# A third tile put ahead of the second halves of the first two, its predecessor's x parked in DRAM, and a new order for the opening

## The chip, the cores and the metric

The kernel runs on one core of a Trainium2 chip. The metric is the device time of one execution in microseconds. TensorE (PE in the rows) multiplies matrices, ScalarE (ACT), VectorE (DVE) and GpSimd (POOL) work on elements, and SyncE (SP) does nothing but issue transfers, in the order of its queue.

## The reference

Three layers follow each other: attention inside chunks of 64 tokens, a layer h·cos(h) of width 2048, and a layer with a softmax gate and a norm of width 1024.

```python
# attention: 8 batches, 8 heads, 576 tokens, head size 64, chunks of 64 tokens
scores = scale * np.matmul(q_c, k_c.transpose(0, 1, 2, 4, 3))
attn = exp(scores - max); attn = attn / (sum(attn) + 1e-09)
x = (attn @ v_c)  ->  4608 tokens x 512
# first layer
h = x @ w_in                     # 512 -> 2048
y = (h * np.cos(h)) @ w_out      # 2048 -> 512
# second layer
h = y @ w_in                     # 512 -> 1024
solu = h * softmax(h)
out = ((solu - mean) / sqrt(var + 1e-06) * g_ln) @ w_out
```

The weights come as 64-bit floats, so that the kernel has to make 32-bit values of them first.

## The kernel before

**Tiles and steps.** The 4608 tokens are 9 tiles j of 512. The first layer is 16 slices f of 128 columns a tile, and a step is one (tile, slice): 144 steps in all. The list `blocks` sets their order: slices 0 to 7 of tile 0, the same of tile 1, then slices 8 to 15 of tile 0, of tile 1, and from step 32 on tile after tile. The sum of a half tile goes to DRAM (`y_part`) and is fetched again (`load_part`) when the second half is done. Halving the first two tiles lets work begin while only half of the weights have been turned into 32-bit values.

**A step.** Every product is made of three passes over a high and a low half of each operand. In a step, PE does 12 products `h` (from `xh`, `xl` and `whi`, `wlo`), ACT rounds h to whole turns (`kt`), DVE takes the rest (`r`), ACT does sine and square (`r<-r`), DVE makes `g`, ACT its high half `gh` and DVE its low half `gl`, and two steps later PE does 12 products `y` out of gh and gl. The first 8 steps use full 32-bit products in place of gh and gl (`gf`).

**Attention.** The tokens are cut into units: 0 to 3 are 128 tokens each (tile 0), all later ones 256, two a tile. Units 0 to 3 are the opening: for each unit q and k are loaded (word `lt`), transposed on PE (`Tq`, `Tk`, tile `qkt`) and copied by ACT (`Cq`, `Ck`), then scores on PE (`S`, tile `sc`), maximum and difference on DVE (`M`, `U`), exponential on ACT (`E`), sums and scaling (`R`, `L` on DVE or `Lp` on POOL), transposes on PE (`P`, tile `pt`) with a copy on ACT (`D`), and the product with v (`V`, tile `x`), which ACT and DVE split into xh and xl (`XH`, `XL`). The word `n` followed by a number is that many products of the identity with itself (tile `none`); nothing reads them.

**The order.** Up to step 33 the whole program is one list of words, written out by hand; each engine does its share of the words in the list's order and never passes one by. From step 34 on a function `step(n)` gives the order, with slots `e`, `p1`, `y`, `a1`, `d1`, `p2`, `a2`, `d2` in which other work is hung by `plan(n, slot, what)`: step n does `mm_in(n)`, slot e, `kt` and `r` of n, `gh` and `gl` of n-1, p1, `mm_out(n-2)`, y, a1, d1, sine and `g` of n, p2, a2, d2. The units of a later tile are hung at step j·16-18 and j·16-10; the scores of a unit and the loads of the next one (`load_next`: 16 transfers for q, 16 for k) are two steps later in slot p2, and its product with v and four loads of the next v nine steps later in p1 (or eight later in p2).

**The blocks of the second layer's weights.** Two halves kk of the second layer's first weights are loaded (`load_blk`) and made into seven blocks. `keep` writes a block's high half (ACT, `wk<-wf` or `wk<-z`) and low half (DVE) into one of the two halves e of the tile `wk`, and stores them to DRAM from SP's queue (`w_w<-wk`, `w_s<-wk`). The next block with the same e can be written only when that store is through. The order is w12 (e=0), w11 (1), w22 (0), s1 (1), s2 (0), s3 (1), s4 (0).

Of the kernel before, what the change touches and what calls it, by code (L numbers as in the profile page):

```python
# [11 lines left out]
F32 = mybir.dt.float32  # L12
F32R = mybir.dt.float32r
# [15 lines left out]
def kernel(  # L29
# [13 lines left out]
    B, H, S, D = q.shape  # L43
# [3 lines left out]
    P = 128  # L47
    CH = 64
    T = 512
    NJ = NT // T  # L50
    SUB = T // P
    NI = NT // P
    KD = DM // P
    NF = F1 // P
# [8 lines left out]
    dr = ctx.enter_context(tc.tile_pool(name="dr", bufs=1, space=DRAM))  # L63
# [10 lines left out]
    NB = 8  # L74

    N32 = NB
    blocks = [(0, 0, NB), (1, 0, NB), (0, NB, NF), (1, NB, NF)]
    blocks += [(j, 0, NF) for j in range(2, NJ)]
    steps = [(j, f) for j, f0, f1 in blocks for f in range(f0, f1)]
    heads = {(j, f0) for j, f0, f1 in blocks}  # L80
    tails = {(j, f1 - 1) for j, f0, f1 in blocks}
    y_part = [dr.tile([P, KD * T], F32, name=f"yp{j}") for j in range(2)]
    y_dram = [dr.tile([2, P, 7 * 256], F32, name=f"yd{j}") for j in range(NJ)]

    xp = ctx.enter_context(tc.tile_pool(name="xp", bufs=2))
# [27 lines left out]
    sync = InOrder(nc.sync, in_order_loads)  # L113
# [110 lines left out]
    def load_w2in(g):  # L224
        t = sp_.tile([P, 1024], U64, tag="st", name="st")
        sync.dma_start(out=t, in_=w_in2[g * P:(g + 1) * P, :])
        raw["in2", g] = t
# [29 lines left out]
    def load_blk(kk):  # L257
        t = sp_.tile([P, 2048], F32, tag="st", name="wf")
        sync.dma_start(out=t, in_=w2f[kk])
        blk[kk] = t, zp.tile([P, 1024], F32, tag="z", name="z"), sp_.tile([P, 2048], F32R, tag="st", name="wk")  # L260
# [144 lines left out]
    def warm(n):  # L405

        t = ps_h.tile([P, P], F32, tag="h", name="none")
        for _ in range(n):
            pe.matmul(out=t, lhsT=ident, rhs=ident, start=True, stop=True)

    def att_tok(i, w):

# [170 lines left out]
    xh, xl = {}, {}  # L583
# [102 lines left out]
    def load_part(j):  # L686
        t = sp_.tile([P, KD, T], F32, tag="st", name="yp")
        sync.dma_start(out=t.rearrange("p m t -> p (m t)"), in_=y_part[j])
        parts[j] = t
# [75 lines left out]
    if True:  # L765
# [48 lines left out]
        for i in range(SUB, NU):  # L814
            j, o = divmod(UNITS[i][0] * CH, T)
# [3 lines left out]
        def plan(n, when, what):  # L819
            att.setdefault((n, when), []).append((lambda i: what(), NU))  # L820

        def conv_at(key, places):
            for (e, k), (n, when) in zip(((0, 0), (0, 1), (0, 2), (1, 0), (1, 1), (1, 2)), places):
                plan(n, when, lambda e=e, k=k: conv(key, e, k))

        for t in (2, 3):
            o = NF * t
            for x in range(2):
                plan(o + 5, "p2", lambda g=2 * x + t - 2: load_w2in(g))
            conv_at(("in2", t - 2), ((o + 7, "a2"), (o + 8, "d2"), (o + 9, "d2"), (o + 8, "a2"), (o + 10, "d1"), (o + 12, "d1")))  # L830
            conv_at(("in2", t), ((o + 13, "a1"), (o + 13, "d1"), (o + 13, "d2"), (o + 13, "a2"), (o + 14, "d2"), (o + 16, "d1")))
        for t in (4, 5):
            o, kk = NF * t, t - 4
            plan(o + 5, "p2", lambda kk=kk: load_blk(kk))
            for what, key, e, n, x in (
# [3 lines left out]
            ):  # L839
                if what == "s":  # L840
                    plan(o + n, f"d{x}", lambda kk=kk, key=key: blk_sum(kk, key))
                else:
                    plan(o + n, f"a{x}", lambda kk=kk, key=key, e=e: keep(kk, e, key, 0))
                    plan(o + n, f"d{x}", lambda kk=kk, key=key, e=e: keep(kk, e, key, 1))
        for t in (6, 7):
            o = NF * t
            for x in range(2):
                g = 2 * (t - 6) + x
                plan(o + 5, "p2", lambda g=g: load_w2out(g))
            g = 2 * (t - 6)  # L850
# [11 lines left out]
        def half_out(n, m):  # L862
# [20 lines left out]
            "Ck": lambda i: att_tokc(i, 1), "S": att_qk, "M": att_max, "U": att_sub, "E": att_exp,  # L883
            "R": att_sum, "L": att_mul, "P": att_pt, "D": att_ptc, "V": att_pv,
            "XH": lambda i: att_x(i, 0), "XL": lambda i: att_x(i, 1),
            "n": warm,
            "nq": lambda i: att_nat(i, "q"), "nk": lambda i: att_nat(i, "k"),
            "cq": lambda i: att_natc(i, "q"), "ck": lambda i: att_natc(i, "k"),
            "tq": lambda i: att_tr(i, "q"), "tk": lambda i: att_tr(i, "k"),
# [223 lines left out]
        BEFORE = 34  # L1113
        ordered[0] = True
        for word in (
# [26 lines left out]
        ).split():  # L1142
            if word == "|":
                first.close()
                cp = act_a.enter_context(tc.tile_pool(name="cp", bufs=2, reuse_waits="tile"))
            else:
                say(word)
# [20 lines left out]
        for n in range(BEFORE - 1, END):  # L1168
            j, f = steps[n - LAG]
# [46 lines left out]
        for i in range(EARLY, NI // 2 + (LAG2 + 1) // 2 + 1):  # L1216
            p, t = i - 1, 2 * i - LAG2
# [98 lines left out]
```

## Time and profile before

| what | value |
|---|---|
| median of 3 runs | 1256.03 us (1254.58 to 1257.68) |
| the profiled execution | 1254.68 us, of which its span is 1252.9 us |
| TensorE busy in the span | 1241.4 us (99%) |
| mean granted TensorE clock | 0.998 |
| VectorE, ScalarE busy | 862.4 us (69%), 751.7 us (60%) |

The span goes from the first to the last instruction; the rest of the profiled execution's time lies around it. A busy engine is not one at its peak, and the ends of TensorE's instructions are modelled, so that starts are compared with starts below.

### The profile page before, as it was taken

What the parts mean: (1) busy time and instruction counts of PE and PEld (TensorE: products, weight loads), DVE (VectorE), ACT (ScalarE), POOL (GpSimd) and SP (SyncE); (2) the same over time, 40 slices, a digit from 0 to 9 for tenths busy, and PEclk for the clock granted to TensorE, in tenths of its full rate; (3) what the DMA queues carried; (4) which work ended last, traced back from release to release, by engine and by line L of the source; (5) the groups of instructions that cost most, each with busy time, mean ns of one, the idle gap of its engine ahead of it and who ended that gap; (6) DMA issues with size and microseconds to landing.
All of it is one profiled execution on the core that took longest, in us unless ns stands there. A gap on an engine that the chain in (4) does not pass through costs nothing.

```text
span 1252.9 us, 20476 instructions
## 1 busy us (share of the span) xinstructions
PE 1241.4 (99%) x7636; PEld 1012.5 (81%) x7636; DVE 862.4 (69%) x1390; ACT 751.7 (60%) x1108; POOL 130.0 (10%) x216
## 2 busy tenths in 40 slices
PE   8999999999999999999999999999999999999998
PEld 7767888888888888888888888888888888888887
DVE  5968875666766766667667757647689777777761
ACT  5968865555645645646646547537666655656552
POOL 1213322011011011011011011000000000000010
PEclk9999999999999999999999999999999999999999
DMA  9952152463263254354373371561556543454325
GB/s 226 276 138 101 58 135 57 114 171 74 54 176 66 58 144 128 85 136 130 80 169 76 85 160 51 194 221 60 164 142 180 129 125 108 121 152 122 75 50 120
DMA packets 249476, 153.95 MB, mean 123 GB/s; under 512 B 180001, under 2 KB 223521, under 8 KB 247585
## 3 DMA queue, kind: packets, MB, share of 16 engines
q1 hardware_dynamic: 245824, 148.32, 45.8%
q0 software_dynamic: 3456, 4.20, 1.5%
q8 instruction: 60, 0.98, 0.4%
q14 instruction: 40, 0.32, 0.1%
q10 hardware_dynamic: 96, 0.13, 0.0%
HBM read 85.73 MB, written 41.68 MB: 102 GB/s over the span
## 4 chain that ended last, share of the span: by engine, by line
PE 96%; ACT 1%; SPq 1%; DMA 1%; DVE 0%; issue 0%; ACTq 0%; DVEq 0%
PE h L104 44%; PE y L104 32%; PE o L104 15%; PE sc L104 2%; PE x L104 2%; SPq L104 1%; DMA qki<-in_k 0%; PE none L104 0%; PE kt L431 0%; PE qt L431 0%; PE pt L104 0%; DMA yd<-ye 0%; PE qkt L104 0%; SPq L1063 0%; ACT lh L104 0%
## 5 line engine op out<-in xcount | busy, mean ns | idle before, releaser
L104 PE MATMUL h<-xh,whi 128*128 128x512 f32 x576 | 229.4, 399 | 0.1
L104 PE MATMUL h<-xl,whi 128*128 128x512 f32 x576 | 224.0, 390 | 0.0
L104 PE MATMUL h<-xh,wlo 128*128 128x512 f32 x576 | 223.9, 390 | 0.0
L104 ACT ACTIVATE kt<-h 128x512 int32<-128x512 f32 x144 | 85.7, 595 | 225.6 <-PE h L104 224.6
L104 PE MATMUL y<-gh,whi 128*128 128x512 f32 x544 | 212.6, 391 | 0.0
L104 PE MATMUL y<-gl,whi 128*128 128x512 f32 x544 | 211.7, 389 | 0.0
L104 PE MATMUL y<-gh,wlo 128*128 128x512 f32 x544 | 211.7, 389 | 0.0
L104 ACT ACTIVATE r<-r 128x512 f32<-128x512 f32 x288 | 181.7, 631 | 47.5 <-DVE r L104 42.9
L104 DVE SCALAR_TENSOR_TENSOR r<-kt,h 128x512 f32<-128x512 int32 x144 | 98.6, 685 | 151.1 <-ACT kt L104 150.9
L104 DVE SCALAR_TENSOR_TENSOR g<-r,h 128x512 f32<-128x512 f32 x136 | 92.7, 681 | 56.0 <-ACT r L104 55.8
L104 PEld LDWEIGHTS h<-xh,whi 128*128 128x128 f32 x576 | 108.0, 188 | 26.0 <-issue 1.6
L104 PEld LDWEIGHTS h<-xh,wlo 128*128 128x128 f32 x576 | 108.2, 188 | 23.3 <-issue 1.2
L104 PEld LDWEIGHTS h<-xl,whi 128*128 128x128 f32 x576 | 108.1, 188 | 22.8
L104 PEld LDWEIGHTS y<-gh,whi 128*128 128x128 f32 x544 | 102.1, 188 | 21.5
L104 PEld LDWEIGHTS y<-gh,wlo 128*128 128x128 f32 x544 | 102.1, 188 | 21.3
L104 PEld LDWEIGHTS y<-gl,whi 128*128 128x128 f32 x544 | 102.1, 188 | 21.0
L104 PE MATMUL o<-whi,lh 128*128 128x512 f32 x288 | 112.0, 389 | 0.0
L104 PE MATMUL o<-wlo,lh 128*128 128x512 f32 x288 | 112.0, 389 | 0.0
L104 PE MATMUL o<-whi,ll 128*128 128x512 f32 x288 | 112.0, 389 | 0.0
L104 ACT ACTIVATE gh<-g 128x512 fp32r<-128x512 f32 x136 | 84.8, 624 | 23.7 <-DVE g L104 17.9
L533 POOL DMA_DIRECT2D ptb<-ptr x96 | 47.2, 499 | 495.4 <-DVE ptr L526 463.1
L104 PE MATMUL h<-whi,yl 128*128 128x512 f32 x252 | 98.2, 390 | 0.2 <-DVE yl L104 0.2
(112 smaller groups left out, 1953.5 us busy)
## 6 DMA issues: line engine op xcount, KB each, us to landing
lt<-bt SPq DMA_DIRECT2D x136, 128.0 KB
yr<-yd SPq DMA_DIRECT2D x18, 896.0 KB
yd<-ts SPq DMA_DIRECT2D x18, 512.0 KB
out<-os SPq DMA_DIRECT2D x142, 64.0 KB
vi<-in_v SPq DMA_DIRECT2D x64, 128.0 KB
qi<-in_q SPq DMA_DIRECT2D x224, 32.0 KB
ki<-in_k SPq DMA_DIRECT2D x224, 32.0 KB
raw<-in_moe_w_in SPq DMA_DIRECT2D x10, 512.0 KB
```

Of the source, the lines that this page charges most:

```text
L104: ins = getattr(self.engine, name)(*args, **kwargs)
L533: (sync if g < 2 else nc.gpsimd).dma_start(out=o[32 * g:32 * (g + 1), c].rearrange("p x s -> p (x s)"), in_=t[32 * c:32 * (c + 1), g].rear ...
```

## The change

Tile 2 is done whole in steps 16 to 31, ahead of the second halves. The second half of tile 1 follows in steps 32 to 39 and that of tile 0 in steps 40 to 47; from step 48 on the order of steps is that of before. There are two buffers for x, so x of tile 0 is written to DRAM (`park`, word `sx.0`, 2 transfers of 1 MB) and read again (`unpark`, `rx.0`). The units of tile 2 (6 and 7) come earlier and the weights of slices 8 to 15 later. The conversion of the second layer's weights is hung 16 steps later (tiles 3 and 4 for 2 and 3), and both halves kk of the blocks are made in tile 5 (steps 80 to 95 and a little beyond), where before they were made in tiles 4 and 5.

```diff
-    blocks = [(0, 0, NB), (1, 0, NB), (0, NB, NF), (1, NB, NF)]
-    blocks += [(j, 0, NF) for j in range(2, NJ)]
+    blocks = [(0, 0, NB), (1, 0, NB), (2, 0, NF), (1, NB, NF), (0, NB, NF)]
+    blocks += [(j, 0, NF) for j in range(3, NJ)]
...
+    x_park = dr.tile([P, 2, KD * T], F32, name="xd")
...
+    def park(j):
+        for e, x in enumerate((xh, xl)):
+            sync.dma_start(out=x_park[:, e], in_=x[j].bitcast(F32).rearrange("p k t -> p (k t)"))
+
+    def unpark(j):
+        for e, (x, name) in enumerate(((xh, "xh"), (xl, "xl"))):
+            x[j] = xp.tile([P, KD, T], F32R, tag=name, name=name)
+            sync.dma_start(out=x[j].bitcast(F32).rearrange("p k t -> p (k t)"), in_=x_park[:, e])
...
-        for t in (2, 3):
+        for j, n in ((1, 38), (0, 46)):
+            plan(n, "p2", lambda j=j: load_part(j))
+        for t in (3, 4):
...
-        for t in (4, 5):
-            o, kk = NF * t, t - 4
-            plan(o + 5, "p2", lambda kk=kk: load_blk(kk))
+        for kk in range(2):
+            o = NF * 5 + 6 * kk
+            plan(o + 5 + kk, "p2", lambda kk=kk: load_blk(kk))
             for what, key, e, n, x in (
-                ("k", "w12", 0, 8, 2), ("s", "s1", 0, 8, 2), ("s", "s2", 0, 9, 2), ("k", "w11", 1, 9, 2),
-                ("k", "w22", 0, 10, 2), ("s", "s4", 0, 12, 1), ("s", "s3", 0, 12, 1), ("k", "s1", 1, 12, 1),
-                ("k", "s2", 0, 12, 2), ("k", "s3", 1, 13, 1), ("k", "s4", 0, 13, 2),
+                ("k", "w12", 0, 7, 2 - kk), ("s", "s1", 0, 7, 2 - kk), ("s", "s2", 0, 7 + (1 - kk), 1 + kk),
+                ("k", "w11", 1, 8 - kk, 2), ("k", "w22", 0, 9 - kk, 1), ("s", "s4", 0, 9 - kk, 2),
+                ("s", "s3", 0, 9 - kk, 2), ("k", "s1", 1, 9 - kk, 2), ("k", "s2", 0, 10 - kk, 1),
+                ("k", "s3", 1, 10 - kk, 2), ("k", "s4", 0, 11 - kk, 1),
             ):
...
-            "lt.0 lt.1 n.9 Tq.0 Cq.0 wi.0 lt.2 Tq.1 Tk.0 lt.3 Ck.0 n.4 S.0 Tk.1 M.0 i0aL U.0 wo.1 E.0 lw.0 Cq.1 R.0 Ck.1 "
+            "lt.0 wi.0 lt.1 Tk.0 lt.2 n.4 lt.3 Tq.0 Cq.0 Ck.0 Tq.1 S.0 Cq.1 wo.1 i0aL Tk.1 M.0 lw.0 n.2 U.0 i0aN E.0 Tk.2 "
```

In the list and in the trace of before there are 40 identity products, in the list of after 20.

TensorE in the opening, from the scores of unit 1 to those of unit 3; before:

```order
L104 MATMUL sc<-qkt 64x64 x16
L104 MATMUL none<-ident 128x128 x3
L104 MATMUL qkt<-ident,qki 128x128 x8
L104 MATMUL pt<-ident,p 128x128 x4
L104 MATMUL none<-ident 128x128 x3
L104 MATMUL sc<-qkt 64x64 x16
L104 MATMUL none<-ident 128x128 x2
L104 MATMUL qkt<-ident,qki 128x128 x4
L104 MATMUL none<-ident 128x128
L104 MATMUL pt<-ident,p 128x128 x4
L104 MATMUL sc<-qkt 64x64 x16
```

And after the change, the same stretch:

```order
L105 MATMUL sc<-qkt 64x64 x16
L105 MATMUL qkt<-ident,qki 128x128 x4
L105 MATMUL none<-ident 128x128 x3
L105 MATMUL qkt<-ident,qki 128x128 x4
L105 MATMUL pt<-ident,p 128x128 x4
L105 MATMUL none<-ident 128x128 x4
L105 MATMUL qkt<-ident,qki 128x128 x4
L105 MATMUL none<-ident 128x128
L105 MATMUL sc<-qkt 64x64 x32
L105 MATMUL none<-ident 128x128
L105 MATMUL pt<-ident,p 128x128 x4
```

The scores of units 2 and 3 now stand together, and the transposes of unit 1's scores (`pt`), which stood ahead of unit 3's scores, stand behind them.

SyncE's queue in tile 5, from the load of v in step 87 on; before (the stores are those of half kk=1; w_w_105 is w12, w_w_104 is w11):

```order
L104 DMA vi<-in_v 64x8x64 x4
L104 DMA qi<-in_q 32x8x32 x16
L104 DMA ki<-in_k 32x8x32 x16
L104 DMA w_w_105<-wk 256x1x512
L104 DMA w_w_104<-wk 256x1x512
L104 DMA w_w_109<-wk 256x1x512
L104 DMA ptb<-ptr 32x256 x8
```

And after (half kk=0; w_w_106 is w12, w_w_105 is w11, w_w_110 is w22, w_s_108 is s1):

```order
L105 DMA vi<-in_v 64x8x64 x4
L105 DMA w_w_106<-wk 256x1x512
L105 DMA qi<-in_q 32x8x32 x16
L105 DMA ki<-in_k 32x8x32 x16
L105 DMA w_w_105<-wk 256x1x512
L105 DMA w_w_110<-wk 256x1x512
L105 DMA w_s_108<-wk 256x1x512
```

The store of w12 has moved ahead of the 32 loads of q and k; that of w11 stands behind them in both.

ScalarE in the same steps; before, from the copy of w12 in step 88 on (`p<-p` is the exponential of a unit's scores):

```order
L104 ACTIVATE wk<-wf 128x512
L104 ACTIVATE kt<-h 128x512
L104 ACTIVATE gh<-g 128x512
L104 ACTIVATE r<-r 128x512 x2
L104 ACT_TABLE_LOAD
L104 ACTIVATE p<-p 128x1024
L104 ACTIVATE wk<-wf 128x512
L104 ACTIVATE kt<-h 128x512
L104 ACTIVATE gh<-g 128x512
```

And after, from the copy of w11 in step 88 on (the second `wk<-wf` is w22, `wk<-z` is s1):

```order
L105 ACTIVATE wk<-wf 128x512
L105 ACTIVATE kt<-h 128x512
L105 ACTIVATE gh<-g 128x512
L105 ACTIVATE wk<-wf 128x512
L105 ACTIVATE r<-r 128x512 x2
L105 ACT_TABLE_LOAD
L105 ACTIVATE p<-p 128x1024
L105 ACTIVATE wk<-z 128x512
L105 ACTIVATE kt<-h 128x512
L105 ACTIVATE gh<-g 128x512
```

Where before the second block (w11) stood ahead of `kt` of step 90, now the fourth one (s1) stands, which writes the half of `wk` that w11's store reads.

## Rows read from the trace of the kernel before

**Rows 1.** The page: busy time, share of the span, instructions.

```profile
PE 1241.4 (99%) x7636; PEld 1012.5 (81%) x7636; DVE 862.4 (69%) x1390; ACT 751.7 (60%) x1108; POOL 130.0 (10%) x216
```

**Rows 2.** TensorE's longest wait by what ended it: total us, times, longest.

```profile
PE qkt L104 <- DMA qki<-in_k: 2.7, 1, 2.7
```

**Rows 3.** Timeline of TensorE in the opening: start us, us, what, idle before.

```profile
1.36 4.21 PE L104 MATMUL none<-ident 128*128 128x128 f32 x18 [1.36 <-POOL ident masks.py:199]
5.36 0.94 PE L104 MATMUL qkt<-ident,qki 128*128 128x128 f32 x4
...
12.56 0.80 PE L104 MATMUL qkt<-ident,qki 128*128 128x128 f32 x4 [2.66 <-DMA qki<-in_k]
13.28 1.13 PE L104 MATMUL sc<-qkt 64*64 64x64 f32 x32
14.35 1.65 PE L104 MATMUL none<-ident 128*128 128x128 f32 x6
15.78 0.85 PE L104 MATMUL qkt<-ident,qki 128*128 128x128 f32 x4
...
21.66 0.69 PE L104 MATMUL sc<-qkt 64*64 64x64 f32 x32
...
31.15 1.19 PE L104 MATMUL h<-xh,whi 128*128 128x512 f32 x4
...
42.03 2.11 PE L104 MATMUL sc<-kt,qt 64*64 64x64 f32 x64 [1.12 <-ACT kt L104]
...
45.48 0.79 PE L104 MATMUL h<-xh,whi 128*128 128x512 f32 x1
```

**Rows 4.** Busy time by stretch: PE, PEld, DVE, ACT, POOL, granted clock, DMA share, GB/s.

```profile
12.88:16.29 3.41, 3.41 (x44) 2.97 (x43) 3.31 (x6) 0.60 (x1) 2.09 (x2) 0.50 1.08 238
...
16.29:31.15 14.86, 13.72 (x268) 11.90 (x266) 11.64 (x25) 11.45 (x22) 1.72 (x3) 1.00 0.89 248
31.15:46.00 14.85, 13.73 (x159) 10.63 (x158) 13.83 (x23) 14.21 (x23) 3.82 (x3) 1.00 1.09 252
```

**Rows 5.** TensorE's groups by shape, the identity products: busy us, mean ns.

```profile
L104 PE MATMUL none<-ident 128*128 128x128 f32 x80 | 14.1, 329 | 1.4 <-POOL ident masks.py:199 1.4
```

**Rows 6.** Timeline of VectorE, the low half of slice 2's weights.

```profile
43.19 0.68 DVE L104 SCALAR_TENSOR_TENSOR wlo<-z,whi 128x512 fp32r<-128x512 f32 x1
```

**Rows 7.** Timeline of SyncE's queue in tile 5, and one q load of tile 2.

```profile
280.06 10.22 SPq L104 DMA_DIRECT2D qi<-in_q  x16
...
554.28 3.83 SPq L104 DMA_DIRECT2D vi<-in_v  x4
558.15 8.02 SPq L104 DMA_DIRECT2D qi<-in_q  x16
566.27 8.62 SPq L104 DMA_DIRECT2D ki<-in_k  x16
574.98 5.03 SPq L104 DMA_DIRECT2D w_w<-wk  x3
```

**Rows 8.** Timeline of VectorE in steps 87 to 91.

```profile
557.14 1.24 DVE L450 STREAM_TRANSPOSE kt<-ki 128x1024 f32<-128x1024 f32 x1
...
564.91 0.68 DVE L104 TENSOR_TENSOR wk<-wf,wk 128x512 fp32r<-128x512 f32 x1
...
579.99 0.69 DVE L104 TENSOR_TENSOR gl<-g,gh 128x512 fp32r<-128x512 f32 x1
```

**Rows 9.** Timeline of ScalarE in steps 89 to 91.

```profile
571.62 0.61 ACT L104 ACTIVATE wk<-wf 128x512 fp32r<-128x512 f32 x1
...
578.12 0.63 ACT L104 ACTIVATE wk<-wf 128x512 fp32r<-128x512 f32 x1 [2.26 <-DMA w_w<-wk]
...
579.13 0.62 ACT L104 ACTIVATE gh<-g 128x512 fp32r<-128x512 f32 x1
```

**Rows 10.** Timeline of TensorE: the first products y of steps 88 and 89.

```profile
571.93 0.39 PE L104 MATMUL y<-gh,whi 128*128 128x512 f32 x1
...
577.37 0.39 PE L104 MATMUL y<-gh,whi 128*128 128x512 f32 x1
```

More of the change, by code (lines that the diff above doesn't have):

```diff
@@ L824, in conv_at @@
                 plan(n, when, lambda e=e, k=k: conv(key, e, k))
-        for t in (2, 3):
+        for j, n in ((1, 38), (0, 46)):
+            plan(n, "p2", lambda j=j: load_part(j))
+        for t in (3, 4):
             o = NF * t
             for x in range(2):
-                plan(o + 5, "p2", lambda g=2 * x + t - 2: load_w2in(g))
-            conv_at(("in2", t - 2), ((o + 7, "a2"), (o + 8, "d2"), (o + 9, "d2"), (o + 8, "a2"), (o + 10, "d1"), (o + 12, "d1")))
-            conv_at(("in2", t), ((o + 13, "a1"), (o + 13, "d1"), (o + 13, "d2"), (o + 13, "a2"), (o + 14, "d2"), (o + 16, "d1")))
-        for t in (4, 5):
-            o, kk = NF * t, t - 4
-            plan(o + 5, "p2", lambda kk=kk: load_blk(kk))
+                plan(o + 5, "p2", lambda g=2 * x + t - 3: load_w2in(g))
+            conv_at(("in2", t - 3), ((o + 7, "a2"), (o + 8, "d2"), (o + 9, "d2"), (o + 8, "a2"), (o + 10, "d1"), (o + 12, "d1")))
+            conv_at(("in2", t - 1), ((o + 13, "a1"), (o + 13, "d1"), (o + 13, "d2"), (o + 13, "a2"), (o + 14, "d2"), (o + 16, "d1")))
+        for kk in range(2):
+            o = NF * 5 + 6 * kk
+            plan(o + 5 + kk, "p2", lambda kk=kk: load_blk(kk))
             for what, key, e, n, x in (
[3 rows of a table removed]
+                ("k", "w12", 0, 7, 2 - kk), ("s", "s1", 0, 7, 2 - kk), ("s", "s2", 0, 7 + (1 - kk), 1 + kk),
+                ("k", "w11", 1, 8 - kk, 2), ("k", "w22", 0, 9 - kk, 1), ("s", "s4", 0, 9 - kk, 2),
+                ("s", "s3", 0, 9 - kk, 2), ("k", "s1", 1, 9 - kk, 2), ("k", "s2", 0, 10 - kk, 1),
+                ("k", "s3", 1, 10 - kk, 2), ("k", "s4", 0, 11 - kk, 1),
             ):
@@ L885 @@
             "XH": lambda i: att_x(i, 0), "XL": lambda i: att_x(i, 1),
-            "n": warm,
+            "n": warm, "sx": park, "rx": unpark,
             "nq": lambda i: att_nat(i, "q"), "nk": lambda i: att_nat(i, "k"),
```

50 rows, old and new, of the table BEFORE are left out of this document.

## Prediction

> **What bounds the kernel now.** I read the page first: TensorE is busy for 1241.4 of 1252.9 us [rows 1], and its other engines have 30 to 40% to spare. Then its waits: the longest is one of 2.7 us for a transfer [rows 2], at 12.56 us; the next is 1.12 us for ScalarE at 42.03 [rows 3]. Behind that, the starts of TensorE follow each other without a wait: a step is 24 products and lasts 5.44 us, as from the first y of step 88 to that of step 89 [rows 10]. So the time is made of three parts: the opening up to the first product h at 31.15 [rows 3], the products themselves, and what holds TensorE up behind 31.15. The change leaves the products of all steps as they are. It can gain in the opening and in the 1.12 us alone, and can lose wherever it makes a new wait. I went through both.
>
> **The opening.** In before, nine identity products fill TensorE from 1.36 on, 4.21 us, 0.47 each [rows 3]. Three later ones took from 14.35 to 15.78, again 0.48 each, and there the granted clock was 0.50, which is 1.2 GHz [rows 3, 4]. At full clock I put them at half, 0.24. Of 40 products 20 go.
>
> Most of them stand where TensorE would wait anyhow. The chain I follow is the scores of units 1 and 3. In before they start at 13.28 and 21.66, 8.38 us apart, and from the second to the first h it is 31.15 - 21.66 = 9.49 us [rows 3]. That last stretch (maximum, exponential, sums, transposes, product with v, split) is passed by the same instructions after the change, so I let h move as far as unit 3's scores do.
>
> Unit 1's scores come later. Their transposes wait for k of unit 2 (12.56), which the new list loads behind the same five loads' worth of bytes. But unit 0's scores have moved back behind both of its copies, and its exponential now stands ahead of the copy of unit 1's k on ScalarE. Worked out: k of unit 0 is there at about 5.4 (the first transposes of before ran at 5.36 without a wait [rows 3]), a set of four transposes 0.94, four products 1.9, four transposes 0.94, two copies of 0.5 make 10.3, then scores 1.1 at 0.50 clock, maximum and difference 0.7 each, exponential and copy 0.5 to 0.6 each: 13.8 instead of 13.28, so +0.5 (the element instructions are put at the 0.6 to 0.7 of their like in [rows 6, 9]). Between them and unit 3's scores there stood nine products, twelve transposes, unit 1's four `pt` and two waits for copies. There remain eight products, twelve transposes and unit 0's `pt`. At the rates of the rows: scores 1.07 (13.28 to 14.35), transposes 0.85, three products 1.43, all at 0.50 clock [rows 3]; then three sets of four at 0.5, five products at 0.24 and the scores of unit 2 at 0.6, at full clock: 3.3. Together 6.7 instead of 8.38. Unit 3's scores and the first h come 8.4 - 6.7 - 0.5 = 1.2 us earlier.
>
> The 1.12 us at 42.03 go too: the product y of step 0 now stands ahead of unit 4's scores and fills the wait. But TensorE then comes to step 2 at 45.48 - 2.3 = 43.2, and the low half of its weights is made by VectorE from 43.19 to 43.87 [rows 3, 6]. From 31.15 to 46 ScalarE was busy 14.21 of 14.85 us and VectorE 13.83 [rows 4]: they set the pace there, not TensorE, and give back what it gains. I let 1.8 of the 2.3 us be given back in the steps up to 60 us; bounds are nothing given back (-2.3) and all (0). **Term: -0.5 us.**
>
> **Parking x.** Two writes and two reads of 1 MB on SP's queue. The read is put at step 33 and its first reader is step 40: 7 x 5.44 = 38 us [rows 10]. The 32 loads of a unit, 1 MB too, took 8.02 + 8.62 us [rows 7]; even at that price two reads take 33 us. **Term: 0**; without the cover it would be the few us by which the read is late. Units 6 and 7 earlier and slices 8 to 15 later exchange element work of like size within steps 8 to 24, where TensorE of before waited for neither: 0.
>
> **The blocks in tile 5.** Here the change adds a wait. In before w12's copy stands in step 88, behind the 32 loads; its store was issued at 574.98, when they were out [rows 7], and ScalarE, which needed that half of `wk` for w22 in step 90, waited until 578.12 [rows 9]. That cost nothing, since gh of step 90 is not needed by TensorE before 577.37 + 5.44 = 582.8 [rows 10]. After the change w12's store goes ahead of the loads and w11's behind them, and the one who needs its half, s1, stands in step 89, in front of kt of step 90 and gh of step 89. gh of step 89 is needed at 577.37: a step less of margin. In the times of before:
>
> - w12's low half: VectorE ends the transpose of step 87 at 557.14 + 1.24, then 0.68 [rows 8]: 559.05. SP, which had the four v loads out at 558.11 [rows 7], stands still until then, and the store takes 0.57 to issue, so that the 32 loads begin at 559.6 and end after 16.7 us [rows 7], at 576.4.
> - w11's store is issued there and through 578.12 - 574.98 = 3.14 later [rows 7, 9]: 579.5. ScalarE had come to that place at 571.62 [rows 9].
> - From s1's copy to the end of gh: 579.13 + 0.62 - 578.12 = 1.63 [rows 9]. So gh of step 89 is ready at 581.2, and y of step 89 starts 3.8 us late [rows 10].
> - VectorE's queue held s1's low half behind it. From ScalarE's copy to the end of gl it was 579.99 + 0.69 - 578.12 = 2.56 [rows 8, 9], so 582.1; the second product y needs it and the first takes 0.23: 0.7 us more. Then VectorE owes an attention sum, s2's low half and g of step 90, which the next h waits for: I put 0.5.
>
> **Term: +5.0 us.** Bounds: if w12's store did not hold SP up, 1.5 less, 3.5; with loads of q and k of 10.22 instead of 8.02 and 8.62 [rows 7], 8.8. I take the rows of this very step. For kk=1 the stores stand behind four v loads alone (3.83 us [rows 7]): 3.83 + 3.14 is 1.5 over a step, within the 4 us of margin that ScalarE has: +0.5, between 0 and 1.5.
>
> **Sum.** 1254.68 - 0.5 + 5.0 + 0.5 = 1259.7 us. The profiled execution is 1.35 under the median of the three runs, 1256.03; on that scale it is 1261.0, which is what I forecast.
>
> **The rivals.**
>
> *The wait in tile 5 stays hidden.* That needs w11's store through by 575.7, which is 1.63 us before 577.37, so the loads faster by 3.8 us than the 16.7 of the rows, or SP ahead of them. For it: the stores and loads of one stretch may overlap better. Against: before's own row has the store issued directly behind the last load. Then 1256.03 - 0.5 + 0.5 = 1256.0, no change.
>
> *The clock stays at half.* With TensorE idle to 5.4 us and 20 products fewer, the granted clock, which in before fell to 0.50 after the wait of 2.66 us [rows 3, 4], may stay there through the opening. Then the 3.3 us of the chain at full clock double, and so does some of the 9.49 us behind them, of which TensorE is on the path for perhaps 2: +3 to +5. For it: from 16.29 to the first h the engine was busy 13.72 of 14.86 us [rows 4], and part of that were products. Against: in the new list no gap behind 5.4 us is as long as 2.66. It gives 1265.
> The Trainium skill, "TensorE: Matmul & The Clock Gate", Part 1, says that the engine starts at half its clock and gets the full one by how busy it has lately been; by that rule the products taken out speak against this change, and the trace agrees as far as its one fall goes.
>
> *The products were the opening.* The 40 took 14.1 us [rows 5]; if TensorE's own queue set the first h, 20 fewer are worth up to 7.0 us. Against: TensorE waited in the opening for a transfer and for copies [rows 2, 3]. With the stall the sum is 1256.03 - 7.0 + 5.5 = 1254.5; faster than before from 5.5 us of gain in the opening on, and by 0.3% only from 9.3 on, or 3.8 where the stall is hidden too.
>
> **How the numbers follow.** Runs of this kernel spread by 3.1 us in 1256; 0.3%, 3.8 us, is about what can be told from no change, so slower begins at 1259.8. The forecast has 0.60 (its own range 1258.5 to 1263.5, three quarters of it beyond 1259.8), hidden 0.18, half clock 0.13, products 0.09. Slower: 0.45 + 0.13 = 0.58; faster: of hidden and products those with the largest gains, 0.06; the rest, 0.36, is the same. The range from 1255.5 to 1265 leaves out the best of the products' case and the worst of the clock's.
>
> **What would show it.** Right: SP's queue in tile 5 has q and k of a unit between the stores of w12 and w11; ScalarE stands idle about 8 us before `wk<-z`, ended by the store; TensorE waits 4 us before a y there, for ScalarE, then under 1 us twice for VectorE; the first h at 29 to 30.5. Wrong: no wait of TensorE around 575 us (hidden), a granted clock of 0.50 beyond 16 us, or a first h under 27.

## The result, and the profile after

| | before | after |
|---|---|---|
| median | 1255.30 us (6 runs, 1254.36 to 1257.68) | 1263.42 us (6 runs, 1261.29 to 1267.15) |
| ratio | 1 | 1.0067, 95% interval 1.0053 to 1.0080 |
| profiled execution, its span | 1254.68, 1252.9 | 1263.98, 1262.2 |

The change makes the kernel slower, by 8.1 us. The page of after, busy time, share and instructions:

```profile
PE 1239.1 (98%) x7596; PEld 1008.5 (80%) x7596; DVE 860.1 (68%) x1389; ACT 752.1 (60%) x1108; POOL 130.6 (10%) x217
```

TensorE works 2.3 us less than in [rows 1] (20 products fewer) in a span that is 9.3 us longer. So the time is in waits. To find them I lay the step starts of both traces side by side (first product `h` of a step, by TensorE's timeline; the experiments further down stand in the same table):

```
us at step           0      36      91      92      97     140
before           31.15  256.97  574.65  580.09  609.79  868.05
after            29.74  255.96  573.64  585.95  619.36  877.62
before + tile 5  31.92  259.11  576.78  589.24  623.58  881.84
stores on POOL   30.21  256.24  573.92  579.36  613.25  871.50
early load       31.04  256.83  574.51  586.56  616.28  874.54
both             30.55  256.19  573.87  579.30  609.01  867.26
both + products  29.23  254.43  572.11  577.55  607.25  865.51
18 in the wait   30.54  255.61  573.29  585.29  618.07  876.33
6 in the opening 29.08  255.19  572.87  585.32  616.40  874.66
no products      30.66  257.71  575.39  588.02  620.11  878.36
```

After is 1.41 us ahead at the first h, 1.01 ahead from step 36 to step 91, then 5.86 behind at step 92 and 9.57 behind at step 97, and no more is lost up to the end. So in these two executions the opening gives 1.01 us, and two places in tile 5 cost 6.87 and 3.71 us. Between steps 4 and 32 the two orders differ, so starts are not compared there.

The opening on TensorE's timeline, the rows that answer to [rows 3]:

```profile
5.18 1.09 PE L105 MATMUL qkt<-ident,qki 128*128 128x128 f32 x4 [5.18 <-DMA qki<-in_k]
...
13.35 0.69 PE L105 MATMUL sc<-qkt 64*64 64x64 f32 x32 [0.22 <-ACT qkt L105]
...
17.89 1.23 PE L105 MATMUL sc<-qkt 64*64 64x64 f32 x64
...
22.25 0.78 PE L105 MATMUL x<-ptb,v 64*64 64x64 f32 x14 [0.60 <-DMA v<-in_v]
...
26.71 0.69 PE L105 MATMUL x<-ptb,v 64*64 64x64 f32 x32 [1.12 <-DVE xl L105]
28.10 0.84 PE L105 MATMUL x<-ptb,v 64*64 64x64 f32 x32 [0.70 <-ACT z L105]
28.87 1.22 PE L105 MATMUL none<-ident 128*128 128x128 f32 x4
29.74 2.05 PE L105 MATMUL h<-xh,whi 128*128 128x512 f32 x4
...
35.58 0.50 PE L105 MATMUL h<-xh,whi 128*128 128x512 f32 x1
...
51.09 0.49 PE L105 MATMUL h<-xh,whi 128*128 128x512 f32 x1 [0.28 <-ACT whi L105]
51.92 0.50 PE L105 MATMUL h<-xh,wlo 128*128 128x512 f32 x1 [0.34 <-DVE wlo L105]
```

Unit 3's scores are the second half of the 64 products at 17.89. The 2.66 us wait for k and the fall of the clock behind it [rows 3, 4] are gone, but the clock falls at another place, and once more in tile 5. The windows of these two falls, in the columns of [rows 4] (the granted clock is the third number from the end):

```profile
28.51:31.92 3.41, 3.41 (x28) 2.91 (x21) 3.38 (x7) 2.45 (x5) 1.64 (x1) 0.50 0.58 206
...
581.47:584.88 3.41, 2.99 (x8) 2.30 (x8) 3.28 (x7) 3.35 (x6) 0.00 (x0) 0.50 0.41 154
```

SP's queue in tile 5, to be read against [rows 7]: w12's store (557.97) now stands ahead of the 32 loads, w11's (576.23) behind them, and the load of the second half's blocks (`wf<-w2f`) stands behind the eight transfers of an exchange (`ptb<-ptr`, which carry a unit's softmax from partition to partition). A row's time is from the start of its first issue to the end of its last, with what SP waits in between.

```profile
557.97 0.59 SPq L105 DMA_DIRECT2D w_w<-wk  x1
558.60 9.64 SPq L105 DMA_DIRECT2D qi<-in_q  x16
568.28 7.85 SPq L105 DMA_DIRECT2D ki<-in_k  x16
576.23 1.23 SPq L105 DMA_DIRECT2D w_w<-wk  x2
...
591.66 5.03 SPq L105 DMA_DIRECT2D ptb<-ptr  x8
596.73 0.58 SPq L105 DMA_DIRECT2D wf<-w2f  x1
```

ScalarE's timeline in the same stretch, the answer to [rows 9]; s1's copy is the row of 579.40:

```profile
579.40 0.63 ACT L105 ACTIVATE wk<-z 128x512 fp32r<-128x512 f32 x1 [8.52 <-DMA w_w<-wk]
579.93 0.58 ACT L105 ACTIVATE kt<-h 128x512 int32<-128x512 f32 x1
580.41 0.62 ACT L105 ACTIVATE gh<-g 128x512 fp32r<-128x512 f32 x1
...
601.91 0.63 ACT L105 ACTIVATE wk<-wf 128x512 fp32r<-128x512 f32 x1 [6.49 <-DMA wf<-w2f]
```

VectorE behind s1's copy:

```profile
580.06 0.69 DVE L105 TENSOR_TENSOR wk<-z,wk 128x512 fp32r<-128x512 f32 x1 [8.92 <-ACT wk L105]
...
581.26 0.69 DVE L105 TENSOR_TENSOR gl<-g,gh 128x512 fp32r<-128x512 f32 x1
...
584.18 0.69 DVE L105 SCALAR_TENSOR_TENSOR g<-r,h 128x512 f32<-128x512 f32 x1
```

TensorE, where [rows 10] has products without a wait; the 585.95 is step 92, the last three rows are the second place:

```profile
581.08 0.50 PE L105 MATMUL y<-gh,whi 128*128 128x512 f32 x1 [4.56 <-ACT gh L105]
582.00 0.79 PE L105 MATMUL y<-gl,whi 128*128 128x512 f32 x1 [0.42 <-DVE gl L105]
...
585.95 0.39 PE L105 MATMUL h<-xh,whi 128*128 128x512 f32 x1
...
604.52 0.50 PE L105 MATMUL h<-xh,whi 128*128 128x512 f32 x1 [1.00 <-DVE g L105]
...
610.83 0.50 PE L105 MATMUL h<-xh,whi 128*128 128x512 f32 x1 [0.57 <-ACT xh L105]
...
613.06 0.50 PE L105 MATMUL h<-xl,whi 128*128 128x512 f32 x1 [1.50 <-DVE xl L105]
```

One chain is to be read through these views: w11's store ends, ScalarE copies s1 (579.40) and then makes gh (580.41), and the product y that needs it starts at 581.08.

### The profile page after: what moved, and what is told of

Read it like the earlier page. It is cut to its first block, busy times and chain, and to the rows that moved or that the text cites. A ratio compares the mean times of both kernels' runs of the same rounds, so it can differ in the third digit from the quotient of the medians.

```text
span 1262.2 us, 20391 instructions
## 1 busy us (share of the span) xinstructions
PE 1239.1 (98%) x7596; PEld 1008.5 (80%) x7596; DVE 860.1 (68%) x1389; ACT 752.1 (60%) x1108; POOL 130.6 (10%) x217
## 4 chain that ended last, share of the span: by engine, by line
PE 79%; issue 12%; SPq 3%; DVE 2%; ACT 2%; DMA 2%; POOL 1%; ACTq 0%; POOLq 0%; DVEq 0%
PE h L105 36%; PE y L105 24%; PE o L105 15%; SPq L105 3%; PE x L105 1%; PE sc L105 1%; DMA w_w<-wk 1%; DMA wf<-w2f 0%; DMA raw<-in_moe_w_in 0%; POOL ptb L543 0%; PE kt L441 0%; PE qt L441 0%; DMA w_s<-wk 0%; PE pt L105 0%; ACT kt L105 0%
```

## The experiments

My theory was that two waits on SP's queue are the whole loss, one for w11's store and one, not yet understood, for what stands in the queue of the second half. The rivals were that tile 2's move or the parking causes it, that ScalarE and VectorE simply have too much to do in these steps, and that TensorE's clock is what costs. Ratios are against the kernel before, run beside each kernel: 1255.48 us, median of 13 runs, for the first two below and for the two with products added to after, 1254.91 us, median of 21, for the other four.

**The schedule of tile 5 alone.** The kernel before, with its tiles, parking and opening untouched, gets only the new places of the conversion and of the blocks:

```diff
-        for t in (2, 3):
+        for t in (3, 4):
...
-        for t in (4, 5):
-            o, kk = NF * t, t - 4
-            plan(o + 5, "p2", lambda kk=kk: load_blk(kk))
+        for kk in range(2):
+            o = NF * 5 + 6 * kk
+            plan(o + 5 + kk, "p2", lambda kk=kk: load_blk(kk))
```

and the new table of blocks.

> The kernel before with one part of the change alone: the conversion of the second layer's weights hung 16 steps later and both halves kk of the blocks made in tile 5. Block order, opening and x stay as before. Theory A (the store of w11 stands behind 32 loads in SyncE's queue, and ScalarE's copy of s1 stands in front of gh of step 89): the whole loss is here, 6.9 us at steps 90 to 92 and 3.7 us at steps 95 to 97, so 1255.3 + 10.5 = about 1265.8 us, ratio 1.0084. Theory B (the loss comes of tile 2 moved ahead, through buffers or x that come late): about 1255.3 us, ratio 1.000.

Measured: 1268.32 us, ratio 1.0101 (1.0084 to 1.0118). ScalarE shows the same two waits:

```profile
582.66 0.63 ACT L104 ACTIVATE wk<-z 128x512 fp32r<-128x512 f32 x1 [8.64 <-DMA w_w<-wk]
...
604.58 0.63 ACT L104 ACTIVATE wk<-wf 128x512 fp32r<-128x512 f32 x1 [5.83 <-DMA wf<-w2f]
```

From step 91 to 92 it loses 589.24 - 576.78 - 5.44 = 7.0 us, and 4.6 more up to step 97 (before takes 29.70 us from 92 to 97). So the loss belongs to the schedule of tile 5, not to tile 2's move or the parking. The median is 2.5 us above what I expected: the second place costs 4.6 us in place of 3.7, and the kernel is already 2.1 us late from step 36 on, ahead of which nothing is edited; that much one execution can differ from another there. The opening, the same words as in before, shows how:

```profile
12.76 0.63 PE L104 MATMUL qkt<-ident,qki 128*128 128x128 f32 x4 [2.76 <-DMA qki<-in_k]
...
20.66 0.69 PE L104 MATMUL sc<-qkt 64*64 64x64 f32 x32
...
31.92 1.21 PE L104 MATMUL h<-xh,whi 128*128 128x512 f32 x4
```

TensorE waits as long for k as in before [rows 3], but the granted clock does not fall behind that wait: it is 1.00 up to 31.92. Unit 3's scores start 1.00 us earlier than in before (20.66, 21.66), and yet the first h comes 0.77 later (31.92, 31.15).

**The stores on another queue.** After, with the stores of `wk` issued by GpSimd, whose queue has no loads of q and k:

```diff
-            sync.dma_start(
+            pool.dma_start(
                 out=w2_dram[key].rearrange("p (x k c) -> p x k c", x=2, k=2)[:, :, kk],
```

> The changed kernel, with the stores of the seven blocks issued by GpSimd in place of SyncE, so that they no longer stand behind the 32 loads. Theory A (order in SyncE's queue): ScalarE's wait of 8.5 us before the copy of s1 goes, TensorE has no wait near 576 us and no fall of its clock there, and the 3.7 us of kk=1 shrink too since its load comes earlier: the opening's gain of 1.0 us is left, about 1254.3 us, ratio 0.999. Theory C (the 16 transfer engines are full of the loads, whichever queue a store is on): the store still lands some 8 us late, time about 1262 us, ratio 1.005. Theory B (too much element work for tile 5): waits of 5 us or more stay in steps 88 to 97.

Measured: 1257.22 us, ratio 1.0017 (1.0008 to 1.0027). The first loss is gone to the last 0.01 us (573.92 to 579.36 is 5.44). The second is not, against what I expected: 4.2 us at steps 96 and 97. Here SP's queue and ScalarE of this run:

```profile
583.48 5.02 SPq L105 DMA_DIRECT2D ptb<-ptr  x8
588.60 0.52 SPq L105 DMA_DIRECT2D wf<-w2f  x1
```

```profile
593.53 0.63 ACT L105 ACTIVATE wk<-wf 128x512 fp32r<-128x512 f32 x1 [4.70 <-DMA wf<-w2f]
```

The second half's load goes out at 588.60, right behind the exchange, and ScalarE, which wants it for the first copy in step 93, stands for 4.70 us. This is a cause of its own.

**The second load ahead of the exchange.** After, with one edit:

```diff
-            plan(o + 5 + kk, "p2", lambda kk=kk: load_blk(kk))
+            plan(o + 5, ("p2", "d1")[kk], lambda kk=kk: load_blk(kk))
```

> The changed kernel with one edit: the second block load of tile 5 (wf of kk=1) is issued at d1 of step 91, ahead of the attention exchange (ptb, 8 transfers, 5.03 us on SP's queue), where it stood at p2 of step 92 behind it. Theory A (the second loss of 3.71 us is this load, which comes one step ahead of its first reader and behind the exchange): ScalarE's wait of 6.49 us for wf is gone or under 2 us, the second loss falls from 3.7 to between 0 and 1.5 us, the first one stays at 6.9, and the median is 1260.5 (1259.5 to 1262). Rival B (the second loss comes from the stores and element work of kk=1 drawn one step together, or from the debt of the first loss): it stays at 3 to 3.7 us, 1263.4.

Measured: 1261.19 us, ratio 1.0051 (1.0038 to 1.0063). TensorE's waits by what ended them (total us, times, longest) and ScalarE's wait for the load:

```profile
PE y L105 <- ACT gh L105: 4.5, 1, 4.5
```

```profile
598.01 0.63 ACT L105 ACTIVATE wk<-wf 128x512 fp32r<-128x512 f32 x1 [1.96 <-DMA wf<-w2f]
```

The wait is 1.96 instead of 6.49 us, which ScalarE's margin bears: from step 92 to 97 it takes 29.72 us, as in before (29.70), while the first loss stays (6.6). The second loss was this load's place, and nothing else had to change for it to go.

**Both edits together.**

> The changed kernel with two edits: the stores of wk go through GpSimd's queue, and wf of kk=1 is loaded ahead of the exchange (d1 of step 91). Theory A (the two queue waits are the whole loss): no step behind 40 loses over 1 us against the kernel before, the granted clock doesn't fall near 580 or 605 us, and the kernel ends 0.5 to 1.0 us ahead of the kernel before, median 1254.5 (1253.8 to 1255.8). Rival B (the second loss is kk=1's element work, not its load): as with the stores moved alone, 1257.2, with 3 to 4 us lost at steps 96 and 97.

Measured: 1253.91 us, ratio 0.9990 (0.9980 to 1.0000), so level with before or a little ahead of it. In the queue the load now leads, 2.2 us ahead of the exchange:

```profile
580.93 0.35 SPq L105 DMA_DIRECT2D wf<-w2f  x1
583.14 5.02 SPq L105 DMA_DIRECT2D ptb<-ptr  x8
```

Every step from 36 to 140 starts 0.78 us ahead of before. The two places are the whole loss.

**Products in the wait.** After, with 18 identity products in TensorE's queue where it waits 4.56 us, to keep the clock up:

```diff
+        plan(91, "p1", lambda: idle(18))
```

(`idle` issues them; the rows count two instructions for each product.)

> The changed kernel, with 18 identity products put into step 91 ahead of the y products of step 89, where TensorE waits 4.6 us anyway; at 0.22 us each they fill 4.0 us of it. If the fall of the granted clock to 0.50 behind the wait costs time of its own (3.4 us at half speed, 1.7 to 1.9 us of products), it does not fall and the time is about 1263.4 - 1.8 = 1261.6 us. If the fall costs nothing because VectorE and ScalarE are what TensorE waits for there, the time stays at 1263.4 us.

Measured: 1263.40 us, ratio 1.0066 (1.0051 to 1.0081), no change. The clock stays at 1.00. TensorE, then VectorE:

```profile
576.01 4.18 PE L105 MATMUL none<-ident 128*128 128x128 f32 x36
581.44 0.50 PE L105 MATMUL y<-gh,whi 128*128 128x512 f32 x1 [1.25 <-ACT gh L105]
...
585.29 0.50 PE L105 MATMUL h<-xh,whi 128*128 128x512 f32 x1
```

```profile
580.42 0.69 DVE L105 TENSOR_TENSOR wk<-z,wk 128x512 fp32r<-128x512 f32 x1 [9.63 <-ACT wk L105]
...
584.55 0.69 DVE L105 SCALAR_TENSOR_TENSOR g<-r,h 128x512 f32<-128x512 f32 x1
```

From s1's low half on VectorE to the next h it is 585.29 - 580.42 = 4.87 us here and 585.95 - 580.06 = 5.89 in after: at full clock h starts as soon as g is there (584.55 + 0.69 = 585.24), at half clock it waits for TensorE's own products y. So the fall costs 1.0 us at this place in after. In this execution s1's low half came 0.36 us later although step 91 began 0.35 earlier, so that the steps show only 0.3 of it (6.56 us lost in place of 6.87), and the medians show none. The clock did not fall in this run's opening either, whose 20 products are those of after.

**Six more products in the opening.**

```diff
-            ... P.3 D.2 XL.1 D.3 i0bN V.2 i1aL ...
+            ... P.3 m.4 D.2 XL.1 D.3 i0bN V.2 m.2 i1aL ...
```

(`m` is `n` with its tile in the other PSUM pool.)

> The changed kernel, with six identity products in two waits of TensorE in the opening, ahead of the products with v of units 2 and 3. The granted clock should then not fall to 0.50 at 28.5 us, and the twelve products of the first h take 2.9 us in place of 3.95, so that step 1 starts 1.0 us earlier. If TensorE's products set the pace of the first steps, the whole time is 1.0 us less, 1262.4 us. If ScalarE and VectorE set it there, the 1.0 us is waited for by step 3 and the time stays at 1263.4 us.

Measured: 1262.24 us, ratio 1.0064 (1.0048 to 1.0081). The clock doesn't fall in the opening. That the six products keep it up is not shown, since with after's 20 alone it did not fall in the opening of *Products in the wait* either. Step 1 starts 1.64 us earlier than in after (33.94, 35.58), but TensorE then waits 1.15 us for weights at 50.37 where after waits 0.28, and at step 36 0.77 are left (255.19). The total stands within the spread of the runs. With the loss in tile 5 in front of it this said little, so I put it on the kernel with both edits:

> The two edits in tile 5 together with six identity products more in the opening (four behind unit 3's pt, two behind unit 2's product with v). If the opening's fall of the clock at 28.5 us cost what the run with the products alone showed (0.8 us by step 36) and nothing gives it back later: 0.8 us less than with the two edits, 1253.7 (1253.0 to 1255). Rival: a gain in the opening is given back by step 92, where VectorE and ScalarE set the pace, 1254.5.

Measured: 1253.26 us, ratio 0.9984 (0.9976 to 0.9993). TensorE at the end of the opening:

```profile
27.83 0.69 PE L105 MATMUL x<-ptb,v 64*64 64x64 f32 x32
28.46 0.71 PE L105 MATMUL none<-ident 128*128 128x128 f32 x4
29.23 1.20 PE L105 MATMUL h<-xh,whi 128*128 128x512 f32 x4
```

The four products h take 1.20 us here, 2.05 in after. This version is faster than both kernels, by 1.7 us against before; its advantage of 0.65 us over both edits alone is as expected, but smaller than the spread of one kernel's openings.

**No products in the opening.** After without its 20:

> The changed kernel without the 20 identity products of the opening. Theory A (they fill waits of TensorE and set nothing but its clock): the first h comes at 29 to 32 us, against 29.74, the granted clock is 0.50 in more of the opening, and the end moves by -0.5 to +2 us: 1263 to 1265.5. Rival (products on the path): the products took 7.7 us in the changed kernel's opening, and the first h comes 2 to 7 us earlier, at 23 to 28, the end 1 to 5 us earlier. Rival (the half clock is what decides): the clock stays at 0.50 beyond 25 us and the first h comes 3 to 6 us later, 1266 to 1269.

Measured: 1264.62 us, ratio 1.0074 (1.0060 to 1.0088); the first h is 0.92 us later than in after.

```profile
13.82 1.13 PE L105 MATMUL sc<-qkt 64*64 64x64 f32 x32
...
19.44 1.87 PE L105 MATMUL sc<-qkt 64*64 64x64 f32 x64
21.24 0.65 PE L105 MATMUL pt<-ident,p 128*128 128x128 f32 x4
...
30.66 2.08 PE L105 MATMUL h<-xh,whi 128*128 128x512 f32 x4 [0.71 <-ACT xh L105]
```

Unit 1's scores take 1.13 us here and 0.69 in after: up to some 20 us the products ran at half their rate. (The views give a clock of 1.00 there; the trace has no entry of the granted clock ahead of 21.04, in after none ahead of 8.03.) Still the first h stands within the 29.74 to 31.04 that it has in the five executions with the 20 products. One run can't exclude that the missing products give what the half clock takes; but h itself waits 0.71 us for ScalarE's xh, so at that point TensorE's own queue did not set the time. Behind 27.86 the clock falls:

```profile
27.86:34.69 6.83, 5.53 (x61) 4.31 (x51) 5.36 (x10) 5.34 (x10) 3.08 (x2) 0.50 0.84 254
```

Step 0 takes 6.72 us in place of 5.84, and step 36 starts at 257.71, 0.88 behind the latest of those five. So for the first h neither the products nor the clock are shown to set the pace; for the steps behind it they may be worth a microsecond, which the medians (1264.62 and 1263.42, after's runs from 1261.29 to 1267.15) can't tell.

**Not tried:** a third buffer for `wk`, which might take the first wait away on SP's own queue. Whether there is room for it beside the other tiles is not shown here.

## Why the prediction was right or wrong

**The direction and the mechanism were right.** The forecast was 1261.0 us, slower, with a stall in tile 5 as the reason; it came out 1263.42, inside the range, and the stall is there as described, from the 8.52 us on ScalarE ended by w11's store to the y that waits for gh. That the schedule alone brings it and that the queue is its cause is shown by two runs. The size was partly luck: the two places cost 10.58 us where the sum had 5.5, and that the time is only 2.4 above the forecast owes 1.9 to the executions that were profiled, before's 1.35 under the median on which the forecast was built and after's 0.56 above its own.

**The opening, -0.5: right in size, by luck.** The first h was forecast 1.2 us earlier, and came 1.41 earlier. But errors cancelled in it. From unit 1's scores (13.35, not 13.8) to unit 3's (half a group behind 17.89, about 18.4) it was 5.1 us in place of 6.7, since the fall of the clock that the sum carried over from [rows 4] did not come there. The stretch from there to h took 11.3 us in place of 9.49, because TensorE waits in it for v, for VectorE and for ScalarE (22.25, 26.71, 28.10). The step that failed is that h moves as far as unit 3's scores do: with the opening of before itself that stretch was 31.92 - 20.66 = 11.26 us in *The schedule of tile 5 alone*, so it was never fixed. The forecast let 1.8 of 2.3 us be given back behind it; of 1.41 and the 1.12 of [rows 3] 1.01 was left at step 36, so 1.5 was given back. But the waits for weights took only 0.62 of this (51.09, 51.92), and the half clock in step 0, which the term had not, some 1.0. The step took 35.58 - 29.74 = 5.84 us; in before, where step 1 starts as in this row, it was 35.99 - 31.15 = 4.84:

```profile
35.99 0.50 PE L104 MATMUL h<-xh,whi 128*128 128x512 f32 x1
```

Of the same opening five executions (after, 18 in the wait, stores on POOL, early load, both) start step 36 between 255.61 and 256.83, so 0.14 to 1.36 us ahead of before; -0.5 and -1.0 can't be told apart.

**Parking, 0: right.** No wait at steps 36 to 48, and the step starts keep their distance of 1.01 through them.

**The first half, +5.0: right in mechanism, 6.87 in size.** Its pieces: y of step 89 was to be 3.8 us late. It started at 581.08 where it stood at 577.37 - 1.01 = 576.36, so 4.72. The loads took 576.13 - 558.60 = 17.5 us, not 16.7. The wait for gl was put at 0.7: the second product y started 0.92 behind the first in place of 0.23, so 0.69. The last piece, 0.5 for g, measured 1.46: without the wait h would have started eleven products behind 582.00, at 584.49, and it started at 585.95. Of this 0.4 is g itself (584.18 + 0.69 = 584.87) and 1.0 the clock, which the sum had forgotten here: I had made a rival of it for the opening and not asked what the stall itself does to it. 4.72 + 0.69 + 1.46 = 6.87.

**The second half, +0.5: mis-sized, and the step failed.** I wrote that for kk=1 "the stores stand behind four v loads alone", and so priced its stores, at 0 to 1.5 us. I didn't price its load. In before both loads stand three steps ahead of their first reader (slots o + 5 and o + 8); after the change it is two steps for kk=0 and one for kk=1, and in that one step SP issues the eight exchange transfers of 5.03 us first; the load, issued at 596.73, then kept ScalarE up to 601.91. That cost 3.71 us. The diff showed it in one line, `o + 5 + kk` beside `7`; I had followed every issue past which a store was moved and none past which the load was.

**The rivals.** *The wait stays hidden* fell: the loads were no faster than the rows. *The clock stays at half* fell in its size: the granted clock was 0.50 from 28.51 to 31.92, which I had named as a sign of being wrong, but over all openings of the new order, with the 20 products, with 26 or with none, the first h stands between 29.08 and 31.04, not 3 to 5 us apart. The rule of the Trainium skill's "TensorE: Matmul & The Clock Gate", Part 1, that the clock goes by how busy the engine has lately been, is what the traces show: it falls after idle stretches (4.56 us ahead of 581.08) and stays where products fill them. It does not go by the program alone: in one and the same opening it fell behind a wait of 2.66 us for k in before [rows 3, 4], and not behind one of 2.76 us in *The schedule of tile 5 alone*. *The products were the opening* fell with the run without them, whose first h came later, not earlier.

**What stays open.** How much the second loss varies: 3.7 us in after, 4.2 with the stores moved (there the clock fell once more, to 0.50 for 3.41 us from 605.35), 4.6 in tile 5 alone, 2.4 without products, 3.1 and 1.4 in the runs with more products, for one and the same load. And one execution's opening differs from another's by 1 to 2 us.

## What to carry to other kernels

When work is drawn together in fewer steps, list for every load and every store in it how many steps lie between issue and first reader, before and after, and what else goes out on that queue in between; one step (5.44 us) behind eight small transfers (5 us) is no lead at all. A store that frees a buffer is a load in this sense: its reader is whoever writes the buffer next. Where the lead can't be had, another queue or a place ahead of the burst gives it back: here two one-line edits took away the whole loss of 8.1 us (1253.91 us, against 1254.91 for the kernel before).

## What was not expected of the hardware

A stall can cost more than its length: behind 4.56 us without products the granted clock was 0.50 for 3.41 us, and the products y followed each other by 0.43 us in place of 0.23, which put 1.0 us on top in this execution. The medians with and without this fall (1263.42, 1263.40) don't differ. Also, sixteen transfers of 32 KB, a unit's q, took 9.64 us on SP's queue, while one store of 512 KB took 0.59 us to issue, so that the time at which w11's store is issued was set by the number of transfers ahead of it, not by their bytes. GpSimd, which took over the fourteen stores, spent 9.9 us more in all (140.5 against 130.6).
